# Three one-pass products of 12-bit halves in place of Strassen's scheme, in a state-space layer followed by a low-rank mixer

## The chip, the cores and the metric

The kernel runs on one core of a Trainium2 chip. The metric is the device time of one execution in microseconds; the median of three runs is given. Times inside an execution come from the hardware profiler, counted from the first instruction.

## The reference

Four batches, eight heads, 768 tokens, head size 32, state size 16. The first part is a chunked state-space scan, the second a mixer over tokens and then over channels (256 wide, inner width 1024):

```
for c in range(nc):                      # chunks of tokens
    M = einsum(C, B) * L                 # L = causal decay, exp(cum_i - cum_j)
    y = M @ x + (C @ state) * exp(cum)
    state = exp(sum la) * state + sum(B * x * decay)
x = y transposed to (batch, tokens, 8*32)
u = x + (x^T @ U @ V)^T                  # low-rank mixing over tokens, rank 32
out = u + max(u @ w_ch1, 0) @ w_ch2      # up, relu, down
```

All is in single precision; the weights U, V, w_ch1 and w_ch2 arrive as 64-bit floats.

## The kernel before, in words

Tokens are taken in pairs of 128-token chunks: 12 pairs `k`, three to a batch (`pairs`, `NPR` = 3). For a pair, `prep` (VectorE) and `decayed` (GpSimd) scale B and C by decays, `turning` transposes them on TensorE, `gram` forms C times B, `mask` (VectorE) applies the causal mask, `intra` and `inter` form y, `state` and `update` carry the state, and `yout` copies y to `yT`, channels by tokens. `ytokening` transposes it back for `project`, whose matmuls are at L595; `mixed` (L606, sums at L610) adds the token mixing to `yT` in place, so that `yT` then holds u.

The two channel products, up (1024 x 256 weight) and down (256 x 1024), are full single-precision matmuls. For batch 0 up is plain (`up`, L710) and the first third of down too (`whole`, L825). For the others both follow Strassen's scheme with seven products per 2 x 2 block: `quad` (L642) multiplies 128 x 128 weights by 384 columns; `down` (L750) multiplies 128 x 128 by 128, four to a product, with u added by transposes against the identity (L746, L819). Sums of the inputs are VectorE's (L617, L621, L739, and `operands` L1017 for the weights), partial results are copied aside by ScalarE (`kept`, L647, L756) and added by VectorE (L651, L764); relu is L630, L685, L715.

The 64-bit weights are turned to single precision by `to_fp32` (L324 to L336): two bit operations `e` and `top` on VectorE, two on ScalarE (`rest`, `power`), then three on VectorE (`rest`, `power`, `w`). Each weight chunk has 512 columns (the first two 256), nine for the two channel weights after one for U and V. `convert` and `convert_ahead` place these pieces between the up products of batch 0.

Nothing is reordered by a scheduler: `manual_schedule` leaves each engine the order in which the program issues. In step k of the main loop (L1032) the up pieces, down pieces and transposes of `plan` and `downs` run first, then `inter(k)`, `gram(k+1)`, `intra(k)`, `state(k+1)`, `mask(k+1)`, `inter`, `yout(k)`, `update(k+1)`. Batch b is projected at k = 3b + 3. All loads are on SP's queue, x and bc in six buffers, the weight words in six. Banks of the accumulator memory are handed out in rings of two under four tags:

```
BANKS = {"w": 2, "x": 2, "z": 2, "y": 2}
```

Of the kernel before, what the change touches and what calls it, by code (L numbers as in the profile page):

```python
# [11 lines left out]
UINT32 = mybir.dt.uint32  # L12
WCOLS = 512
NWORDS = 6
# [6 lines left out]
def kernel(  # L21
# [28 lines left out]
    P = 128  # L50
# [10 lines left out]
    HT = HS // P  # L61
# [5 lines left out]
    raw = ctx.enter_context(tc.tile_pool(name="raw", bufs=6))  # L67
# [40 lines left out]
    x_sb, bc_sb, paced = {}, {}, []  # L108
# [7 lines left out]
    def load_bc(k, blocks=(0, 1)):  # L116
        b, q = pairs[k]
        if k not in bc_sb:
            bc_sb[k] = raw.tile([P, 2, 2, NH, N], FP32, tag="bc", name="bc")
        for c in blocks:  # L120
            for i, src in enumerate((B, C)):
                paced.append(nc.sync.dma_start(
                    out=bc_sb[k][:, i, c],
                    in_=src[b, :, ts(2 * q + c, P), :].rearrange("h s n -> s h n")))

    def load_x(k, blocks=(0, 1)):
        b, q = pairs[k]
        if k not in x_sb:
            x_sb[k] = raw.tile([P, 2, NH, D], FP32, tag="x", name="x")
        for c in blocks:  # L130
            paced.append(nc.sync.dma_start(
                out=x_sb[k][:, c],
                in_=x[b, :, ts(2 * q + c, P), :].rearrange("h s d -> s h d")))
# [6 lines left out]
    w1 = const.tile([P, NCB, DF], FP32)  # L140
    w2 = const.tile([P, NM, DM], FP32)

    w2b = [[w2[:, half * NM // 2:(half + 1) * NM // 2, ts(n, P)] for n in range(2)]
           for half in range(2)]
    w2s = [const.tile([P, NM // 2, P], FP32, name=f"w2s{i}") for i in range(4)]
    weights = []

    def words_of(dst):
        p, i, j = dst.shape
        t = raw.tile([P, 2 * WCOLS], INT32, tag="words", name="words", bufs=NWORDS)  # L150
        weights.append((dst, t[:p, :2 * i * j]))
        return t[:p, :2 * i * j]

    def load_words(dst, src):

        p, i, j = dst.shape
# [4 lines left out]
    for k in range(NPR):  # L161
# [4 lines left out]
        if k:  # L166
            load_x(k)
    t = words_of(UV)
# [6 lines left out]
    eighths = words_of(w1[:, :, :quarter])  # L175
    weights.pop()
    for k in range(2):
        dst, t = w1[:, :, ts(k, P)], eighths[:, ts(k, 2 * NCB * P)]
# [3 lines left out]
    held += [load_words(w1[:, :, ts(k, quarter)], w13[:, :, ts(k, 2 * quarter)])  # L182
# [3 lines left out]
    for m in range(0, NM, 2):  # L186
        load_words(w2[:, m:m + 2],
                   w22[m * P:(m + 2) * P].rearrange("(m p) d -> p m d", p=P))
    for k in range(NPR + 1, NB * NPR):
        del paced[:-2]  # L190
        load_bc(k)
        load_x(k)
        if k > NPR + 3:
            for i in range(2, len(paced)):
                hold(paced[i], paced[i - 2])


# [110 lines left out]
    def to_fp32(dst, words):  # L308

        p, i, j = dst.shape
# [3 lines left out]
        def tmp(name, dtype):  # L318
            t = att.tile([P, WCOLS], dtype, tag=name, name=name)
            return t[:p, :i * j]  # L320

# [13 lines left out]
                                       op0=ALU.bitwise_and, op1=ALU.bitwise_or)  # L335
        nc.vector.scalar_tensor_tensor(  # L336
            out=dst, in0=rest.rearrange("p (i j) -> p i j", i=i), scalar=2.0 ** -20,
            in1=power.bitcast(FP32).rearrange("p (i j) -> p i j", i=i),
            op0=ALU.mult, op1=ALU.mult)
        yield  # L340

# [209 lines left out]
    def yout(k):  # L551
        b, q = pairs[k]
        if q == 0 and b:
            yT[b] = mix.tile([P, NCB, S], FP32, tag="yT", name="yT")
            ytok[b] = mix.tile([P, NC, DM], FP32, tag="ytok", name="ytok")
# [27 lines left out]
    def mixer(b):  # L583
        uT = yT[b]
        pT = mix.tile([P, P], FP32, tag="pT", name="pT")
        gT, hold, relus = {}, {}, []
# [14 lines left out]
        def mixed():  # L601
# [6 lines left out]
            for q in (0, 2, 1, 3):  # L608
                u = block(q // 2, q % 2)
                nc.vector.tensor_tensor(out=u, in0=h[q][:, :HS], in1=u, op=ALU.add)  # L610
            t = hold["t"] = [mix.tile([P, HS], FP32, tag=f"t{i}", name=f"t{i}",
                                      bufs=2 if i == 2 else 1) for i in range(4)]
            for i, (l, r) in enumerate((
                    (block(0, 1), block(0, 0)), (block(1, 1), t[0]),
                    (block(0, 1), block(1, 1)), (t[1], block(1, 0)))):
                if b:
                    nc.vector.tensor_tensor(out=t[i], in0=l, in1=r, op=ALU.subtract)  # L617

        def difference():

            nc.vector.tensor_tensor(out=hold["t"][2], in0=block(0, 1), in1=block(1, 1),  # L621
                                    op=ALU.subtract)
# [4 lines left out]
        def relu(n=None):  # L627
            for _ in range(len(relus) if n is None else min(n, len(relus))):
                g = relus.pop(0)
                nc.scalar.activation(g, g, AF.Relu)  # L630

        def quad(i):

            X = {}
            if i == 0:
                for k in range(2):
                    gT[k] = mix.tile([P, NM, HS], FP32, tag="gT", name="gT")

            def times(name, tag, lhsT, rhs, start=True):
                if start:  # L640
                    X[name] = bank(tag, HS)
                nc.tensor.matmul(out=X[name], lhsT=lhsT[:, ts(i, P)], rhs=rhs, start=start,  # L642
                                 stop=True, skip_group_check=True)

            def kept(name, of):
                X[name] = att.tile([P, WCOLS], INT32, tag=name, name=name).bitcast(FP32)[:, :HS]
                behind.setdefault("part", nc.scalar.copy(out=X[name], in_=X[of]))  # L647

            def out(k, half, of, other):
                g = gT[k][:, half * NM // 2 + i]  # L650
                nc.vector.tensor_tensor(out=g, in0=X[of], in1=X[other], op=ALU.add)  # L651
                relus.append(g)

            def p1():
                times("x", "x", w1[:, 0, :DF // 2], block(0, 0))
                kept("e", "x")
                relu(1)

            def p5():
                times("y", "z", ws[:, 0], hold["t"][0])  # L660
                kept("power", "y")
                relu(1)

            def p2():
                times("z", "z", w1[:, 1, :DF // 2], block(1, 0))
                out(0, 0, "z", "e")

            def p6():
                times("x", "x", ws[:, 1], hold["t"][1], False)
                kept("top", "x")  # L670
                relu(1)

            def p3():
                times("y", "z", ws[:, 3], block(1, 1), False)
                out(1, 0, "y", "top")

            def p7():
                times("x", "x", ws[:, 2], hold["t"][2], False)
                out(1, 1, "x", "power")

            def p4():
                times("x", "x", ws[:, 4], hold["t"][3], False)
                if i == 3:
                    relu()
                nc.vector.tensor_relu(gT[0][:, NM // 2 + i], X["x"])  # L685

            return dict(zip((1, 5, 2, 6, 3, 7, 4), (p1, p5, p2, p6, p3, p7, p4)))

        def two(i):

            q, r = quad(i), quad(i + 1)
            start = [q[1], q[5], q[2], q[6], q[3], None] if i else [
                q[1], q[5], None, q[6], q[3], q[2]]
            return start + [q[7], r[1], r[5], q[4], r[6], r[3], None, r[7], r[2], None, r[4]]

        def quads():

            q = [quad(i) for i in range(NM // 2)]
            when = {1: 0, 5: 1, 6: 3, 3: 4, 2: 5, 7: 6, 4: 9}
            order = sorted((7 * i + t, i, m) for i in range(NM // 2) for m, t in when.items())  # L700
            order = [q[i][m] for _, i, m in order]
            order.insert(2, None)
            return order

        def up(k, m):
            if m == 0:
                gT[k] = mix.tile([P, NM, HS], FP32, tag="gT", name="gT")
            g = bank("xz"[k if b == 0 else m % 2], HS)
            for n in range(NCB):
                nc.tensor.matmul(out=g, lhsT=w1[:, n, ts(m, P)], rhs=uT[:, n, ts(k, HS)],  # L710
                                 start=(n == 0), stop=(n == NCB - 1))
            if m % 2 and b:
                nc.vector.tensor_relu(gT[k][:, m], g)
            else:
                nc.scalar.activation(gT[k][:, m], g, AF.Relu)  # L715

        def down(j):

            X, S = {}, []

            def blocks():
                return [[gT[k][:, half * NM // 2:(half + 1) * NM // 2, ts(j, P)]
                         for half in range(2)] for k in range(2)]

            def sums(lo=0, hi=NM // 2, which=range(4), flush=True):
                if flush:
                    relu()
                if not S:
                    for _ in range(2):
                        t = raw.tile([P, 2 * WCOLS], INT32, tag="words", name="words",  # L730
                                     bufs=NWORDS).bitcast(FP32)
                        S.extend(t[:, ts(v, NM // 2 * P)].rearrange("p (i t) -> p i t", t=P)
# [379 lines left out]
```

## Time and profile before

| | us |
|---|---|
| median of three runs (238.43 to 241.82) | 239.74 |
| span of the profiled execution, first to last instruction | 237.3 |
| TensorE busy in it | 227.2 |
| TensorE weight loads busy (beside the products) | 175.1 |
| VectorE busy | 154.1 |
| ScalarE busy | 95.9 |
| GpSimd busy | 20.0 |

The profile gives no time of the profiled execution other than its span. PE is TensorE, PEld its weight loads, DVE VectorE, ACT ScalarE, POOL GpSimd, SP the queue that issues transfers. A line in a timeline begins with its start in us and the duration in us, then engine, source line, operation, output and inputs, shape and count; in brackets stands how long the engine was idle before and what ended the wait. Durations of neighbours overlap, so the distance between starts is the price of an instruction in a stream. A matmul in single precision leaves two records.

### The profile page before, as it was taken

To read this page: it belongs to the slowest core of one execution; us is meant where nothing else is said; L and a number is where in the kernel's file an instruction comes from. 1 tells how busy PE (TensorE), PEld (TensorE's weight loads), DVE (VectorE), ACT (ScalarE), POOL (GpSimd) and SP (SyncE) were. 2 spreads that over 40 slices of the span, in tenths; PEclk is the share of its full clock that TensorE was granted. 3 is DMA by queue.
4 is the path that set the end of the run, shared out by engine and by line. 5 is a ranking of instruction groups with operands and counts; after the bars stand their busy time and mean duration, and the time that the engine had idled before them with its cause. 6 is when DMAs were issued, how large, how long until landed. Compare 5 with 4: busy or idle time off the path is not lost.

```text
span 237.3 us, 7378 instructions
## 1 busy us (share of the span) xinstructions
PE 227.2 (96%) x3166; PEld 175.1 (74%) x3166; DVE 154.1 (65%) x363; ACT 95.9 (40%) x247; POOL 20.0 (8%) x40
## 2 busy tenths in 40 slices
PE   7699899997999999999999999999999999999995
PEld 5367556664878988565799987565799896559994
DVE  3666899878798575576896572566965362478411
ACT  5435658674705212456514112466312014652110
POOL 4221001122020200011012000010000000000000
PEclk9979999997999999999999999999999999999999
DMA  5985969996455556600001011000001001000111
GB/s 77 112 98 145 276 79 337 136 116 77 63 53 71 70 59 72 179 3 3 3 3 48 4 44 44 4 3 0 3 3 47 28 18 44 0 0 3 44 47 46
DMA packets 81909, 14.60 MB, mean 62 GB/s; under 512 B 76052, under 2 KB 80084, under 8 KB 81876
## 3 DMA queue, kind: packets, MB, share of 16 engines
q1 hardware_dynamic: 81876, 14.13, 32.6%
q8 instruction: 25, 0.41, 0.7%
q14 instruction: 8, 0.07, 0.1%
HBM read 10.98 MB, written 3.15 MB: 60 GB/s over the span
## 4 chain that ended last, share of the span: by engine, by line
PE 88%; DVE 5%; SPq 2%; DMA 1%; issue 1%; ACT 1%; DVEq 0%; ACTq 0%
PE x L750 17%; PE x L642 14%; PE z L750 13%; PE z L642 10%; PE x L710 5%; PE z L710 5%; PE y L546 3%; PE y L524 3%; PE x L414 2%; PE x L825 2%; PE w L566 2%; PE w L595 2%; PE w L447 2%; PE w L383 1%; DMA bc<-in_C_dram 1%; DVE M L426 1%
## 5 line engine op out<-in xcount | busy, mean ns | idle before, releaser
L642 PE MATMUL x<-t,ws 128*128 128x384 f32 x72 | 28.7, 496 | 0.0
L750 PE MATMUL x<-w2s,words 128*128 128x128 f32 x176 | 23.3, 276 | 0.0
L750 PEld LDWEIGHTS x<-w2s,words 128*128 128x128 f32 x176 | 21.6, 193 | 0.0
L630 ACT ACTIVATE gT<-gT 128x384 f32<-128x384 f32 x36 | 19.0, 528 | 2.4 <-DVE gT L651 2.3
L474 POOL TENSOR_TENSOR Sm<-S,slot 128x256 f32<-128x256 f32 (+1 forms) x12 | 8.8, 731 | 120.3 <-DVE S L467 89.2
L642 PEld LDWEIGHTS x<-t,ws 128*128 128x128 f32 x72 | 12.5, 190 | 8.0 <-ACT top L647 1.3
L739 DVE TENSOR_TENSOR words<-gT 128x512 f32<-128x512 f32 (+1 forms) x28 | 16.7, 597 | 0.6 <-ACT gT L630 0.6
L651 DVE TENSOR_TENSOR gT<-z,top 128x384 f32<-128x384 f32 x12 | 6.7, 558 | 15.2 <-PE z L642 13.4
L647 ACT COPY e<-x 128x384 f32<-128x384 f32 x12 | 5.7, 478 | 23.1 <-PE x L642 23.1
L808 ACT COPY o<-x 128x128 f32<-128x128 f32 x11 | 2.9, 265 | 28.6 <-PE x L750 28.6
L426 DVE TENSOR_TENSOR M<-x,causal 128x256 int32<-128x256 int32 x23 | 8.7, 419 | 8.6 <-PE z L414 7.3
L710 PE MATMUL x<-yT,w 128*128 128x384 f32 x32 | 13.2, 539 | 0.6 <-DVE yT L610 0.6
L558 ACT COPY yT<-y 128x256 f32<-128x256 f32 x24 | 7.8, 376 | 13.9 <-PE y L524 13.9
L467 DVE SCALAR_TENSOR_TENSOR S<-S,kept,w 128x64 f32<-128x64 f32 x40 | 11.2, 279 | 2.6 <-PE w L447 0.8
L353 DVE TENSOR_TENSOR BC<-bc,F 128x512 f32<-128x512 f32 (+1 forms) x15 | 9.2, 621 | 5.4 <-DMA bc<-in_C_dram 3.6
L750 PE MATMUL x<-w,gT 128*128 128x128 f32 x88 | 12.6, 286 | 0.0
L685 DVE TENSOR_SCALAR gT<-x 128x384 f32<-128x384 f32 x12 | 6.7, 557 | 9.1 <-PE x L642 9.1
L750 PEld LDWEIGHTS x<-w,gT 128*128 128x128 f32 x88 | 10.8, 191 | 2.3 <-issue 1.6
L710 PE MATMUL z<-yT,w 128*128 128x384 f32 x32 | 12.1, 504 | 0.0
L750 PE MATMUL z<-w2s,words 128*128 128x128 f32 x88 | 11.9, 279 | 0.0
L524 PE MATMUL y<-T,Sm 32*64 32x64 f32 x352 | 11.2, 233 | 0.7 <-ACT settled L480 0.4
L750 PE MATMUL z<-w,gT 128*128 128x128 f32 x88 | 11.6, 276 | 0.0
(186 smaller groups left out, 503.2 us busy)
## 6 DMA issues: line engine op xcount, KB each, us to landing
words<-in_moe_w_ch_dram SPq DMA_DIRECT2D x7, 512.0 KB, 5.9
x<-in_x_dram SPq DMA_DIRECT2D x24, 128.0 KB, 3.5
out_dram<-o SPq DMA_DIRECT2D x11, 256.0 KB, 2.1
bc<-in_B_dram SPq DMA_DIRECT2D x24, 64.0 KB, 2.9
bc<-in_C_dram SPq DMA_DIRECT2D x24, 64.0 KB, 2.8
words<-in_moe_w_ch_dram SPq DMA_DIRECT2D x2, 256.0 KB, 4.0
words<-in_moe_V_dram SPq DMA_DIRECT2D x1, 192.0 KB
words<-in_moe_U_dram SPq DMA_DIRECT2D x1, 192.0 KB, 5.2
```

The lines of the kernel that those rows point to most:

```text
L353: nc.vector.tensor_tensor(out=st[k]["BC"][:, :, c:c + n].rearrange("p i c h n -> p i (c h) n"), in0=bc_sb[k][:, :, c:c + n].rearrange("p i ...
L426: done = nc.vector.tensor_tensor(out=M[:, r].bitcast(INT32).rearrange("p c s i -> p (c s) i"), in0=g[r].bitcast(INT32).rearrange("p c s i ...
L467: done = nc.vector.scalar_tensor_tensor(out=new, in0=st["S", b], scalar=kept[:, b, j, None], in1=add, op0=ALU.mult, op1=ALU.add)
L474: nc.gpsimd.tensor_tensor(out=s["Sm"][:, sl], in0=s["S"][:, sl].rearrange("p i (s d) -> p i s d", s=2), in1=slot[:, None, :, None].to_broa ...
L524: product = nc.tensor.matmul(out=y[p][ts(r % 2, H), r // 2, c], lhsT=own[ts(r, Q)], rhs=s["T"][ts(r, Q), 1, c, ts(p, H)], start=fresh(k, p ...
L546: nc.tensor.matmul(out=y[p][ts(i, Q), n, c], lhsT=x_sb[k][half, c, h], rhs=s["M"][half, h // 2, c, h % 2], start=fresh(k, p, [i]), stop=Tr ...
L558: nc.scalar.copy(out=yp[:, :, :, p], in_=st[k]["y"][p])
L630: nc.scalar.activation(g, g, AF.Relu)
L642: nc.tensor.matmul(out=X[name], lhsT=lhsT[:, ts(i, P)], rhs=rhs, start=start, stop=True, skip_group_check=True)
L710: nc.tensor.matmul(out=g, lhsT=w1[:, n, ts(m, P)], rhs=uT[:, n, ts(k, HS)], start=(n == 0), stop=(n == NCB - 1))
L739: nc.vector.tensor_tensor(out=S[v][:, lo:hi], in0=l[:, lo:hi], in1=r[:, lo:hi], op=op)
L750: nc.tensor.matmul(out=X[name], lhsT=lhsT[:, i], rhs=rhs[:, i], start=start and u is None and i == 0, stop=True, skip_group_check=True)
```

## The change

Strassen's scheme goes, with all its sums. Each operand of the up and down products is held as three arrays in a reduced single-precision type: `near` (the upper 12 bits), `low` or `far` (the remainder, scaled or not) and `both` (a combination of the two). A product is a sum of three products near x near, low x far, both x both, with the accumulator scaled by 1 + 2^-12 on ScalarE between the first two and the third. Tokens are taken in blocks of 256, three to a batch: `split(j)` makes the three arrays of u, `up(j, i)` two of eight row blocks, `down(j)` 256 tokens of output. Weight conversion gets a fourth and fifth step, `weight(c)` runs steps 3 and 4 of chunk c, steps 1 and 2 of chunk c+1, then step 5 of chunk c. x and bc have four buffers instead of six, words eleven, and x and bc of step k+4 are loaded in step k.

```diff
-NWORDS = 6
+NWORDS = 11
+NEAR = 1.0 - 2.0 ** -13
+EPS = 2.0 ** -12
...
-    raw = ctx.enter_context(tc.tile_pool(name="raw", bufs=6))
+    raw = ctx.enter_context(tc.tile_pool(name="raw", bufs=4))
...
-    w1 = const.tile([P, NCB, DF], FP32)
-    w2 = const.tile([P, NM, DM], FP32)
+    w1 = [const.tile([P, NCB, DF], FP32R, name=f"w1{i}") for i in range(3)]
+    w2 = [const.tile([P, NM, DM], FP32R, name=f"w2{i}") for i in range(3)]
...
+        if parts:
+            near, low, both = parts
+            far = wide(tmp("top", FP32))
+            nc.scalar.activation(near, w, AF.Copy, scale=NEAR)
+            nc.gpsimd.tensor_tensor(out=far, in0=w, in1=near.bitcast(FP32), op=ALU.subtract)
+            yield
+            nc.scalar.activation(low, far, AF.Copy, scale=1.0 / EPS)
+            nc.vector.scalar_tensor_tensor(out=both, in0=near.bitcast(FP32), scalar=-EPS,
+                                           in1=far, op0=ALU.mult, op1=ALU.add)
+            yield
...
+        def split(j):
...
+            nc.scalar.activation(parts[0], u, AF.Copy, scale=NEAR)
+            nc.gpsimd.tensor_tensor(out=parts[1], in0=u, in1=parts[0].bitcast(FP32),
+                                    op=ALU.subtract)
+            nc.vector.scalar_tensor_tensor(
+                out=parts[2], in0=parts[1].bitcast(FP32), scalar=-1.0 / EPS,
+                in1=parts[0].bitcast(FP32), op0=ALU.mult, op1=ALU.add)
...
+        def scaled(t):
+            nc.scalar.activation(t, t, AF.Copy, scale=1.0 + EPS)
...
+            def first():
+                X["t"] = bank("xz"[i % 2], 2, W)
+                for m in range(2):
+                    products(X["t"][:, m], terms(2 * i + m, (0, 1)), m == 0)
+                scaled(X["t"])
+
+            def second():
...
+                for m in range(2):
+                    products(t[:, m], terms(2 * i + m, (2,)), False)
+                near, far, both = [g[:, ts(i % 2, 2)] for g in gs[j, i // 2]]
+                nc.scalar.activation(near, t, AF.Relu, scale=NEAR)
+                nc.vector.scalar_tensor_tensor(out=far, in0=t, scalar=0.0, in1=near.bitcast(FP32),
+                                               op0=ALU.max, op1=ALU.subtract)
+                nc.vector.scalar_tensor_tensor(
+                    out=both, in0=far.bitcast(FP32), scalar=-1.0 / EPS, in1=near.bitcast(FP32),
+                    op0=ALU.mult, op1=ALU.add)
...
+        def down(j, tag="z"):
...
+            def first(k):
+                if k == 0:
+                    X["t"] = bank(tag, 2, DM)
+                products(X["t"][:, k], terms(k, (0, 1)), k == 0)
+                if k:
+                    scaled(X["t"])
+            def second():
...
+                    products(t[:, k], terms(k, (2,)), False)
+                o = mix.tile([P, 2, DM], FP32, tag="o", name="o")
+                nc.scalar.copy(out=o, in_=t)
...
+            return lambda: first(0), lambda: first(1), second
...
+    split(0)
+    weight(1)
+    weight(2)
...
+    ups[0, 0][0]()
+    weight(3)
+    ups[0, 0][1]()
+    ups[0, 1][0]()
...
+        if k == NPR:
+            pieces = ([lambda: weight(6), ups[1, 0][0], lambda: weight(7), ups[1, 0][1],
+                       ups[1, 1][0], lambda: weight(8), ups[1, 1][1]] + turns[:2]
+                      + [lambda: weight(9)] + turns[2:])
...
+        elif q == 0:
...
+            pieces = ([d[0]] + tokens + [d[1], project] + turns[:2]
+                      + [mixed, lambda s=split: s(0), d[2]] + turns[2:] + u)
+        else:
...
+            pieces = ([lambda s=split, q=q: s(q)] if k > NPR + 2 else []) + (
+                [d[0]] + tokens + [d[1], u[0], d[2]] + u[1:-3] + turns[:2] + u[-3:-1] + turns[2:]
+                + u[-1:])
...
+        load(k + NPR + 1)
...
+    for j in range(1, NBL):
+        split(j)
+        d = downs[j - 1]
+        u = staggered([ups[j, i] for i in range(NQ)])
+        run([d[0], u[0], d[1], u[1], u[2], d[2]] + u[3:])
+    run(downs[NBL - 1])
```

`staggered` orders four up units as f0, f1, s0, f2, s1, f3, s2, s3, where f is a unit's `first` and s its `second`; d[0], d[1], d[2] are the three parts of a down block.

## The prediction

> **What bounds the kernel now.** I read the chain of waits first, then the page's slices, then the stages by windows, then the pitches in the timelines.
>
> The chain of waits, by engine:
>
> ```profile
> PE 88%; DVE 5%; SPq 2%; DMA 1%; issue 1%; ACT 1%; DVEq 0%; ACTq 0%
> ```
>
> TensorE sets the end; but a share is a mean over stages. The slices show where that is close:
>
> ```profile
> PE   7699899997999999999999999999999999999995
> DVE  3666899878798575576896572566965362478411
> PEclk9979999997999999999999999999999999999999
> ```
>
> In slices 6 to 14 (30 to 83 us) VectorE is as full as TensorE. The windows from the end of batch 0's token mixing, cut where loop steps k=3 and k=6 begin, then at the three projections (L595), say it in microseconds (window, length, then PE, PEld, DVE, ACT, POOL busy, clock, DMA):
>
> ```profile
> 29.40:51.70 22.30, 21.69 (x140) 13.62 (x141) 19.57 (x44) 15.59 (x35) 2.43 (x4) 1.00 0.90 173
> 51.70:75.40 23.70, 21.99 (x530) 17.07 (x528) 20.72 (x44) 10.83 (x26) 3.67 (x4) 0.93 0.57 68
> 79.75:132.25 52.50, 52.49 (x784) 41.32 (x788) 36.25 (x82) 20.13 (x52) 4.40 (x6) 1.00 0.28 48
> 132.25:183.54 51.29, 51.23 (x714) 39.82 (x718) 29.88 (x69) 17.50 (x46) 1.14 (x2) 1.00 0.05 18
> 183.54:237.30 53.76, 50.91 (x380) 42.05 (x379) 25.37 (x56) 15.49 (x42) 0.00 (x0) 1.00 0.08 25
> ```
>
> First two rows: VectorE 88% busy with the weights' conversion. Last three: TensorE alone, VectorE 47 to 69%. The change takes work off TensorE everywhere and adds VectorE, ScalarE and GpSimd work, so the two halves must be costed apart.
>
> TensorE's pitch is the distance between starts (up, down, transpose):
>
> ```profile
> 205.68 1.45 PE L642 MATMUL x<-t,ws 128*128 128x384 f32 x4
> 206.97 0.81 PE L642 MATMUL z<-yT,ws 128*128 128x384 f32 x2
> 217.01 1.06 PE L750 MATMUL z<-w,words 128*128 128x128 f32 x8
> 217.90 0.27 PE L746 MATMUL x<-ident,yT 128*128 128x128 f32 x1
> 218.01 1.06 PE L750 MATMUL x<-w2s,words 128*128 128x128 f32 x8
> ```
>
> A product has two records: 384 columns 1.29/4 = 322.5 ns each, 128 columns 0.89/8 = 111.7. A transpose is one, 110 ns. The line through both is 6 ns + 0.823 ns a column and record, so 2 clocks of 2.4 GHz a record and 4 a product. Loading 128 columns of weights shows in neither, so it is hidden.
>
> VectorE in one quarter of the first weight (512 columns):
>
> ```profile
> 33.06 0.42 DVE L324 TENSOR_SCALAR e<-words 128x512 int32<-128x512 int32 x1
> 33.40 0.42 DVE L326 TENSOR_SCALAR top<-words 128x512 int32<-128x512 int32 x1
> 33.73 0.68 DVE L332 SCALAR_TENSOR_TENSOR rest<-top,rest 128x512 f32<-128x512 f32 x1
> 34.33 0.68 DVE L334 SCALAR_TENSOR_TENSOR power<-words,power 128x512 int32<-128x512 int32 x1
> 35.05 0.69 DVE L336 SCALAR_TENSOR_TENSOR w<-rest,power 128x512 f32<-128x512 f32 x1
> 35.66 0.42 DVE L324 TENSOR_SCALAR e<-words 128x512 int32<-128x512 int32 x1
> ```
>
> Start to start: 0.34, 0.33, 0.60, 0.72, 0.61, together 2.60 us; a two-source instruction on 512 floats is priced 0.62. For 256 columns the same view gives 1.55 and 0.35. GpSimd's two-source instruction at 128, 192 and 256 columns:
>
> ```profile
> 14.40 0.40 POOL L365 TENSOR_TENSOR bd<-bc,FD 128x128 f32<-128x128 f32 x1 [0.65 <-DMA bc<-in_B_dram]
> 21.81 0.51 POOL L474 TENSOR_TENSOR Sm<-S,slot 128x192 f32<-128x192 f32 x1 [2.73 <-DVE S L467]
> 18.46 0.61 POOL L474 TENSOR_TENSOR Sm<-S,slot 128x256 f32<-128x256 f32 x1 [1.90 <-DVE S L467]
> ```
>
> Estimate from these for 512: 0.61 + 256 x 1.7 ns = 1.05 us; beside a busy VectorE the 256 form takes 1.06 (65.65), so up to 1.8.
>
> **The Trainium skill.** "FP8 and Floating Point Precision", TensorE Precision Notes: true FP32 takes four passes, reduced precision reads the float and truncates it. Four clocks a column agree; no row here shows the reduced form. "TensorE: Matmul & The Clock Gate", Back-to-back issue gap: N/2.4 + 2.5 ns for one pass, 109 ns at 256. The same page says the clock halves after idling; here, after 1.29 us without work at 54.13, four L710 records took 2.72 us instead of 1.29. "VectorE: DVE Perf Modes", the errata section: (N+151)/0.96, 691 ns for a two-source fp32 instruction of 512; L332 and L336 last 680 to 690.
>
> **The change, part by part.**
>
> *TensorE.* One pass over 256 columns, by my line at one clock: 6 + 256 x 0.412 = 111 ns (bounds: 107 of pure streaming; 216 at two clocks a column). An up block is 8 row blocks x 3 x 2 = 48 products, a down block 2 x 3 x 8 = 48: 5.33 us each. A batch of three blocks: 32.0 plus 12 transposes 1.3 = 33.3. Now it is 28 x 0.645 + 84 x 0.2234 + 1.3 = 38.2. It saves 4.9 a batch; batch 0 (32 x 0.645, 16 x 0.433, 56 x 0.2234, transposes) saves about 8. All: 22.7 us.
>
> *VectorE after the mixing.* Up to the end of the last conversion its queue holds: mixing sums 4 x 0.47 = 1.9; two splits 1.2; two 256 chunks 3.8 less 0.4 done before, seven 512 chunks x (2.60 + 0.62 for `both`) = 22.5; six up units x two evacuations x 0.62 = 7.4; `keep` 0.9; three `prep` 1.8; one `mask` (4 x 0.34) and one `update` 2.5. That is 41.6 us of pure occupation. It leaves out Strassen's operands and sums, which lay later. (Before, the conversion stood in the same queue with no evacuations: relu was ScalarE's.)
>
> *New waits.* `both` waits for `far` on GpSimd, which waits for `near` on ScalarE: 0.64 (L1019) + 1.05 + two handovers of 0.1 = 1.9. Only `e` and `top` of the next chunk (0.67) stand between, so VectorE idles 1.2 in each of six chunks, 1.9 in the last, 0.8 and 0.6 in the halves: 10.5. Behind the waiting `both` stand the evacuations of the up products, and TensorE waits for those through the banks. `split(0)`: 1.1. An evacuation's `near` is queued on ScalarE behind `low`, which waits for GpSimd too: 0.5 x six units = 3.0. Sum 14.6.
>
> *Stage sums* against the profiled 237.3. Mixing at 29.4, unchanged. Then 41.6 + 14.6 = 56.2: 85.6. The first down product needs the last chunk's `low`; ScalarE's `settled` and VectorE's mask stand before it: 86.7. Before, this point (k=4) was 56.15; TensorE had hidden there. k=4: down 5.33 + 0.44, two up units 2.67, four token and four turn transposes 0.88, attention 2.65 (154.51 to 157.16), waits 1.3 (`gram` 1.1 and a scaling 0.2, below): 13.3. k=5: 5.77 + 5.33 + 0.88 + 2.65 + 1.3 = 15.9. k=6 to the projection: 4.0. Waking the clock: 1.7. Together 34.9, and the projection of batch 1 comes at 121.6 instead of 79.75.
>
> Each later batch: 51.9 (mean of two windows) - 4.9 + new waits. These are, each step: `gram`'s fourth bank is freed by the last unit's `near` and `far` (0.55 + 0.62 + handovers, less `inter` 0.37), 1.1 where it is 0.4 now: 0.7 x 3. Mixing to the first up product: two sums 0.94, `near` 0.6, GpSimd 1.05, handovers 0.3, under a cover of 2.4 (d2 and turns), 0.8, and 0.4 for pT. The last `second` of a block follows its scaling by 0.44 only: 0.2 to 0.3 x 3. Together 4.0. Two batches 2 x 51.0 = 102.0: 223.6. In the other steps `split` stands on GpSimd behind `Sm` and `bd` (0.61 each): by the step's start plus 3.7 it is done, and the first up product comes 4.0 after it, behind d0, tokens and d1: nothing, and up to 1 us a step if GpSimd runs at its slow rate.
>
> The tail from the last projection: 1.45 + 0.45 + 0.87, d2 2.2, split 0.8, three ups 16.0, three downs 17.3, waits 3.6 (scaling before the last d2 0.8, splits and g 2.8), copy 0.5, store 2.1, handovers 0.3: 45.6, against 53.8 now. End: 269.2.
>
> *At nothing:* x and bc prefetched by four buffers instead of six, loads moved into the loop on SP behind the stores: k+4 is asked for two steps of 15 us before `prep`, landing is 3.5 us. If that cover goes (a store ahead of it waits for its copy), 3.5 a step. The words no longer wait for six buffers, which takes away waits of 2.3 us for bc.
>
> The median of the runs shown lies 2.4 above the span (the page has no other time of that execution), so 271.6.
>
> **Rivals.**
> *Handovers pace the ups.* An up unit is 1.33 on TensorE, 1.24 on VectorE and about 1.0 on ScalarE. If PSUM-sourced evacuations cost 0.70, VectorE needs 1.4; with the scaling's latency each of 36 units gains 0.4: 285. For: the three are nearly level. Against: downs stand between most of them.
> *The waits hide.* All the new ones (14.6, 8.0, 3.6 and 4.3 in k=4 and k=5) at zero: 238.7 + 2.4 = 241. For: TensorE is in order but deep. Against: VectorE and ScalarE run in order too and nothing stands between.
> *Not one pass.* At 216 ns, 1152 x 0.105 = 121 us, of which the six units under the conversion hide 30: 362. No row excludes it.
> *TensorE stays the bound (faster).* Place: the 29.4 to 86 stretch. If VectorE's queue did not count there, 237.3 - 22.7 + 2.4 = 217. It decides once the conversion ends 31.9 earlier, near 54; VectorE's 41.6 us of instructions end at 71 without any wait, so they would have to cost 40% less than measured.
>
> **The numbers.** My forecast 0.60 (own range 258 to 284), handovers 0.22, waits hidden 0.08, not one pass 0.05, TensorE-bound 0.05. By a bound of 2% (about what a measurement of this kernel tells from no change): faster 0.05, within 0.08, slower 0.87. Range 252 to 290: it leaves out the last three, 0.18.
>
> **What would show it.** Records of 256 columns one per product at about 111 ns; the first L595 after batch 0's at 118 to 125; VectorE waiting for GpSimd's `far` about 1.2 us per chunk; TensorE half idle from 35 to 87; later projections 51 apart. A first projection below 100 proves the conversion's price wrong; 45 apart, the waits.

## The result, and the profile after

| | us |
|---|---|
| median before (four runs) | 239.81 |
| median after (300.11 to 303.39) | 302.57 |
| ratio, with its 95% interval | 1.263 (1.254 to 1.273) |
| span of the profiled execution, before and after | 237.3 and 301.0 |

Some executions take over 1.5% longer than the fastest of their kernel, and the medians here and below leave those out. The kernel is slower, as forecast, but by 63 us instead of 32, and 13 us above the range. The slices after, and the chain of waits by engine:

```profile
PE   8988265653343988989989899699898989999994
DVE  4675766667667226073393664735619172555450
PEclk9999557565555695988999999999799999999999
PE 51%; DVE 17%; SPq 11%; ACT 10%; POOL 4%; issue 4%; DMA 2%; POOLq 0%; ACTq 0%; DVEq 0%
```

TensorE was 88% of the chain and is 51%. From slice 5 to 13 (30 to 98 us) it is mostly a third to two thirds busy, and its clock is at 0.5 to 0.7. VectorE is not full there either, 6 or 7 tenths: the two wait for each other. Here are the same stages as before, by windows (from the mixing to the first down product, from there to the projection of batch 1, then from projection to projection and to the end):

```profile
29.60:98.85 69.25, 32.21 (x313) 25.97 (x313) 45.46 (x89) 31.60 (x62) 15.25 (x15) 0.56 0.42 70
98.85:141.54 42.69, 38.97 (x543) 36.25 (x541) 17.21 (x34) 15.68 (x33) 5.88 (x7) 0.83 0.26 39
141.54:197.96 56.42, 51.38 (x846) 46.52 (x845) 31.22 (x60) 24.39 (x49) 8.27 (x9) 1.00 0.21 35
197.96:252.06 54.10, 50.32 (x775) 45.79 (x774) 26.84 (x50) 22.18 (x43) 4.93 (x5) 0.97 0.05 17
252.06:301.00 48.94, 42.93 (x377) 39.55 (x376) 21.25 (x31) 20.29 (x36) 3.84 (x3) 1.00 0.07 23
```

The projection of batch 1 comes at 141.5 instead of 79.75: 61.8 of the 63.7 us (about 8 us less of batch 0's down products are left by then than before). The two periods are 3.9 and 2.8 longer, the tail 4.9 shorter.

Inside the first window, one quarter of a weight on VectorE, the conversion's `far` on GpSimd, and the next evacuation:

```profile
39.06 0.69 DVE L338 SCALAR_TENSOR_TENSOR rest<-top,rest 128x512 f32<-128x512 f32 x1
39.66 0.68 DVE L340 SCALAR_TENSOR_TENSOR power<-words,power 128x512 int32<-128x512 int32 x1
40.38 0.69 DVE L343 SCALAR_TENSOR_TENSOR e<-rest,power 128x512 f32<-128x512 f32 x1
...
43.12 0.69 DVE L354 SCALAR_TENSOR_TENSOR w<-w,top 128x512 fp32r<-128x512 f32 x1 [1.38 <-POOL top L351]
44.27 0.69 DVE L676 SCALAR_TENSOR_TENSOR words<-x,words 128x512 fp32r<-128x512 f32 x1 [0.46 <-ACT words L675]
...
41.81 1.27 POOL L351 TENSOR_TENSOR top<-e,w 128x512 f32<-128x512 f32 x1 [3.13 <-ACT w L350]
```

`both` (L354) stood waiting 1.38 us for GpSimd, as the forecast's 1.2 said; GpSimd took 1.27 for 512 columns instead of the 1.05 drawn on from narrower ones. The next lines show the products' pitch in a dense stretch at the end, and the same sixteen down products in step k=4 and near the end:

```profile
286.05 1.11 PE L645 MATMUL x<-u,w 128*128 128x256 f32 x8
287.00 1.58 PE L645 MATMUL z<-u,w 128*128 128x256 f32 x12
288.41 0.63 PE L645 MATMUL x<-u,w 128*128 128x256 f32 x4
...
98.85 3.78 PE L645 MATMUL x<-w,words 128*128 128x256 f32 x16
...
250.06 2.07 PE L645 MATMUL x<-w,words 128*128 128x256 f32 x16
```

There is one record a product, at 1.41/12 = 117.5 ns (113 to 118 in other dense stretches): one pass, as the change says. At 98.85 sixteen of them took twice as long, after the clock had fallen in the idle start. The largest sum of waits on TensorE, the longest single ones on it, and VectorE's for GpSimd (waiter, what it waited for, sum, times, longest):

```profile
PE z L430 <- DVE words L676: 12.7, 8, 3.7
PE x L645 <- ACT w L350: 9.7, 3, 5.5
DVE w L354 <- POOL top L351: 12.3, 9, 2.1
```

The first is `gram` waiting for the bank of the last up unit, in eight steps; the second are three up units of batch 0 waiting for `near` of their weights.

SP's queue has 11% of the chain instead of 2%. The moved loads do not explain the loss: SP's part of the chain ends at 49 us, no load in the list of waits holds TensorE after the first microseconds, and VectorE waited for loads 0.5 us in all (3.6 before).

### The profile page after: what moved, and what is told of

Its sections match the earlier page's. It is cut to its first block, busy times and chain, and to the rows that moved or that the text cites. A ratio compares the mean times of both kernels' runs of the same rounds, so it can differ in the third digit from the quotient of the medians.

```text
span 301.0 us, 7915 instructions
## 1 busy us (share of the span) xinstructions
PE 241.5 (80%) x3438; PEld 211.9 (70%) x3438; DVE 158.7 (53%) x322; ACT 128.0 (43%) x262; POOL 44.6 (15%) x61
## 4 chain that ended last, share of the span: by engine, by line
PE 51%; DVE 17%; SPq 11%; ACT 10%; POOL 4%; issue 4%; DMA 2%; POOLq 0%; ACTq 0%; DVEq 0%
PE x L645 30%; SPq L129 8%; PE z L645 8%; DVE words L676 5%; DVE words L678 4%; ACT words L675 3%; POOL top L351 3%; PE y L562 2%; DMA bc<-in_C_dram 2%; PE z L430 2%; ACT z L650 2%; POOL u L636 2%; SPq L138 2%; PE y L540 1%; SPq L164 1%
## 5 line engine op out<-in xcount | busy, mean ns | idle before, releaser
L645 PE MATMUL x<-w,words 128*128 128x256 f32 x576 | 82.5, 294 | 1.3 <-issue 1.1
L645 PEld LDWEIGHTS x<-w,words 128*128 128x128 f32 x576 | 73.8, 197 | 3.1 <-issue 1.2
L645 PE MATMUL x<-u,w 128*128 128x256 f32 x288 | 48.5, 306 | 21.2 <-ACT w L350 9.7
L645 PEld LDWEIGHTS x<-u,w 128*128 128x128 f32 x288 | 40.7, 205 | 25.4 <-ACT w L350 10.8
L645 PE MATMUL z<-u,w 128*128 128x256 f32 x288 | 46.6, 305 | 7.2 <-ACT z L650 3.7
L645 PEld LDWEIGHTS z<-u,w 128*128 128x128 f32 x288 | 40.1, 205 | 10.7 <-ACT z L650 6.2
L676 DVE SCALAR_TENSOR_TENSOR words<-x,words 128x512 fp32r<-128x512 f32 x24 | 16.6, 691 | 57.5 <-ACT words L675 57.5
L650 ACT ACTIVATE x<-x 128x512 f32<-128x512 f32 x36 | 21.0, 584 | 44.4 <-PE x L645 44.4
L678 DVE SCALAR_TENSOR_TENSOR words<-words 128x512 fp32r<-128x512 f32 x48 | 35.4, 736 | 1.6
L430 PE MATMUL z<-Cm,T 32*64 32x128 f32 x184 | 14.2, 339 | 12.7 <-DVE words L676 12.7
L676 DVE SCALAR_TENSOR_TENSOR words<-z,words 128x512 fp32r<-128x512 f32 x24 | 16.5, 688 | 9.2 <-ACT words L675 9.1
L430 PE MATMUL x<-Cm,T 32*64 32x128 f32 x184 | 17.2, 336 | 0.2
L351 POOL TENSOR_TENSOR top<-e,w 128x512 f32<-128x512 f32 (+1 forms) x9 | 10.4, 1153 | 35.6 <-ACT w L350 35.6
L708 ACT COPY o<-x 128x512 f32<-128x512 f32 x12 | 7.0, 586 | 19.1 <-PE x L645 19.1
```

The source lines that it names most:

```text
L351: nc.gpsimd.tensor_tensor(out=far, in0=w, in1=near.bitcast(FP32), op=ALU.subtract)
L430: nc.tensor.matmul(out=g[r][cols, c], lhsT=s["T"][rows, 0, c, cols], rhs=s["Cm"][rows, :, c, cols], start=(c == 0), stop=True, skip_group_ ...
L645: nc.tensor.matmul(out=t, lhsT=lhsT, rhs=rhs, start=start, stop=True, skip_group_check=True)
L650: nc.scalar.activation(t, t, AF.Copy, scale=1.0 + EPS)
L676: nc.vector.scalar_tensor_tensor(out=far, in0=t, scalar=0.0, in1=near.bitcast(FP32), op0=ALU.max, op1=ALU.subtract)
L678: nc.vector.scalar_tensor_tensor(out=both, in0=far.bitcast(FP32), scalar=-1.0 / EPS, in1=near.bitcast(FP32), op0=ALU.mult, op1=ALU.add)
```

## The experiments

My theory after the result was that the start is a chain of handovers in which VectorE waits, TensorE idles and its clock falls, and that the later steps wait for the evacuation. The rival was that products and evacuations simply cost more than forecast. Each run below begins with its median; the kernel before stood at 236.7 to 239.3 beside these runs.

Positions come from one profiled execution each. In these the mixing itself began anywhere from 28.6 to 35.6 us, at code that the edits leave alone. So they are counted from the first sum of the mixing, which stands at 29.56 in the changed kernel. "d0" is the first down product (69.3 on this count) and "P1" the projection of batch 1 (112.0). A period is the time from one projection to the next.

**No split of the weights.**

```diff
-    w1 = [const.tile([P, NCB, DF], FP32R, name=f"w1{i}") for i in range(3)]
+    w1 = [const.tile([P, NCB, DF], FP32R, name="w1")] * 3
...
-            near, low, both = parts
-            far = wide(tmp("top", FP32))
-            nc.scalar.activation(near, w, AF.Copy, scale=NEAR)
...
-            nc.scalar.activation(low, far, AF.Copy, scale=1.0 / EPS)
```

> The weights are not split: near, low and both are one array, so the fourth and fifth conversion steps (ScalarE, GpSimd, VectorE) are left out and the products are of other numbers. Theory start (the chain of ScalarE, GpSimd and VectorE per weight chunk sets the time up to the first down product): VectorE loses 12.3 us of waits and 5 us of instructions, the first down product comes 17 us earlier than 98.9, near 82, the clock recovers sooner, total 280 to 286. Theory products (the pitch of 118 ns and the evacuations set the time, the start only shows it): total within 5 us of 302.

278.4; d0 50.2, P1 88.7. That is 24 us less. d0 comes 19.1 us sooner, and the stage from d0 to P1 is 4.2 us shorter at a clock of 0.96 instead of 0.83. The periods (55.4, 53.0) fell by 1 us each and the tail (49.1) stayed. So the split of the weights costs about 19 us in the start. But d0 in this kernel still comes 23 us later than the same point in the kernel before (26.8), so the split is not the only cost. VectorE waits here too, 6.1 us for ScalarE before the evacuations, whose `near` now stands behind the next chunk's `power`.

**`far` on VectorE.** `nc.gpsimd.tensor_tensor(out=far` becomes `nc.vector.tensor_tensor(out=far`.

> The subtraction that gives far in the conversion is VectorE's instead of GpSimd's. Theory start, handover form: a chunk's wait of 1.4 us goes, an instruction of 0.62 comes and about 0.1 of waiting for near remains, 0.7 us a chunk gained: 5 us earlier at the first down product, total about 297. If VectorE's amount of work and not the waiting set the start, 0.62 x 8 = 5 us are lost: 307.

303.0; d0 69.1, as good as unchanged. In this execution the mixing began 6.0 us later than in the changed kernel (35.58 instead of 29.56), before any edited instruction:

```profile
35.58 0.56 DVE L626 TENSOR_TENSOR yT<-x,yT 128x384 f32<-128x384 f32 x1 [2.89 <-PE z L622]
...
104.64 3.78 PE L645 MATMUL x<-w,words 128*128 128x256 f32 x16
...
DVE words L676 <- ACT words L675: 6.5, 6, 2.3
DVE top L351 <- ACT w L350: 5.8, 9, 0.7
```

VectorE's 12.3 us of waiting for GpSimd became 5.8 us of waiting for `near` (`e` and `top` no longer cover it), about 5 us of forming `far` itself, and 1.9 us more of waiting before the evacuations. So neither outcome came, 5 us sooner or 5 later. Not GpSimd is the price, but whatever stands between `w` and `both` with nothing beside it. The next stage, whose code is the same, took 3.9 us less at a clock of 0.95; why the clock stayed up there is not shown.

**Idle matmuls against the clock's fall.** `fill(12)` or `fill(16)` ahead of batch 0's up units and of `state(4)`, `fill(8)` ahead of `gram` at k=4 and 5.

> Idle matmuls are put before the up products of batch 0 and before the waits of steps k=3, 4 and 5, so that TensorE's clock does not fall; nothing else changes. Theory clock: steps k=4 and k=5 take 17.3 us each like the later ones instead of 18.6 and 19.8, and VectorE's wait for the decay products in the start shrinks: 4 to 6 us gained, total about 297. Theory start without the clock: 302, or some microseconds more where an idle matmul outlasts the wait it fills.

294.8; d0 68.6, d0 to P1 37.1 instead of 42.7, at a clock of 1.00 instead of 0.83. So about 5.6 us of this stage were the clock's. In the start the clock rose as well, from 0.56 to 0.82, and d0 came only 0.7 us sooner, so there it was not the price, or the idle matmuls took back what it gave. On the stage after d0 other runs agree: the stage took 38.2 us at 0.96 and 40.4 at 0.89, with its products unchanged.

**Early transposes.** This is the edit of the later steps; k=3 and k=4 are changed likewise.

```diff
-                [d[0]] + tokens + [d[1], u[0], d[2]] + u[1:-3] + turns[:2] + u[-3:-1] + turns[2:]
-                + u[-1:])
+                [d[0]] + tokens + [d[1], u[0]] + turns + [d[2]] + u[1:])
```

> The transposes of the pair after next, and with them ScalarE's copies T and Cm (1.3 us), are placed ahead of the last up units of a step instead of between their parts. Theory: gram waits for the last unit's evacuation because its near stands behind T and Cm on ScalarE; at k = 4, 5, 7, 8 gram comes 1.2 us sooner, and at k=3 state no longer waits 4.2 us for Cm: 6 to 9 us gained, total 294 to 296. Rival: the last evacuation is late because VectorE paces the units (1.42 us each against 1.41 on TensorE): less than 2 us gained.

297.9, between the two expectations; but `gram`'s waits for VectorE fell only from 12.7 to 11.5, and 2.5 us of the gain lie where the granted clock was higher (0.87 instead of 0.83 between d0 and P1, 1.00 instead of 0.97 in the second period). VectorE's queue shows why the early transposes helped `gram` so little (`far` L676, `both` L678):

```profile
164.59 0.69 DVE L676 SCALAR_TENSOR_TENSOR words<-x,words 128x512 fp32r<-128x512 f32 x1 [4.75 <-ACT words L675]
165.32 0.69 DVE L678 SCALAR_TENSOR_TENSOR words<-words 128x512 fp32r<-128x512 f32 x1
165.99 0.69 DVE L676 SCALAR_TENSOR_TENSOR words<-z,words 128x512 fp32r<-128x512 f32 x1
166.72 0.69 DVE L678 SCALAR_TENSOR_TENSOR words<-words 128x512 fp32r<-128x512 f32 x1
```

It runs without a gap from the first unit on, a unit in 1.33 to 1.40 us, and is idle 4.75 before. TensorE issues a unit in 1.36 to 1.41 with four in a row, so VectorE's tail reaches into `gram`. As to `gram`, the rival of this run stands.

**VectorE's order.** Early transposes; `both` of a unit issued after the next unit's `far`; `u[1], u[2]` ahead of `d[2]`.

> The early transposes of the run before, and on VectorE each unit's both is issued after the next unit's far (the last one after mask), and the last part of a down block goes after the first unit's second instead of before it. Theory (VectorE's two instructions a unit, 1.42 us, are what gram waits for): gram's wait falls from 1.2 to 4 us a step to under 1, in the steps k = 5 to 10, 8 to 10 us gained over the early transposes alone: 288 to 290. Rival (TensorE's own work fills the step and gram's wait is only its end): under 2 us.

295.4; d0 66.4, d0 to P1 38.2 (67.6 and 41.4 in the run before). The periods are 55.6 and 52.5 instead of 56.1 and 52.9 there: 1.0 us, where 8 to 10 were expected in the steps k=5 to 10. The 3.2 us between d0 and P1 come with the clock, 0.96 instead of 0.87. TensorE is busy 49.2 of 52.5 us in the second period, so little is left for the order of VectorE to give.

**No third product.** Both x both is left out in up and down.

> The third product of up and down (both x both) is left out, 384 of 1152 matmuls of 118 ns, 45 us of TensorE; all evacuations stay. If TensorE sets the later steps, the distance between projections falls by 96 x 118 ns = 11.3 us from 55.3 to 44, and the total by about 38. If VectorE's evacuations set them, units come at 1.42 us of VectorE whatever TensorE does, and the distance falls by half of that or less.

292.3, in one execution; the others took 297.1 to 300.1, and the profile is of one of these. The mean clock was 0.80 to 0.81 in all of them (0.86 to 0.89 in the changed kernel). There are ninety-six products less in a batch, and the periods are 57.8 and 53.3. Their window lines:

```profile
137.77:195.53 57.76, 48.64 (x750) 43.29 (x749) 30.98 (x60) 23.76 (x49) 8.23 (x9) 0.79 0.21 34
195.53:248.87 53.34, 42.52 (x679) 37.90 (x678) 26.66 (x50) 20.96 (x43) 4.96 (x5) 0.87 0.05 16
```

Work of 11 us a batch was taken from TensorE and its clock fell to 0.79 and 0.87. `gram`'s waits for VectorE in the two periods rose from 5.2 to 13.1 us. This run therefore does not say what the steps would cost at the full clock; it shows that most of a gain on TensorE can be lost to waits and clock, 10 us of an expected 38 being left.

**No third array from the evacuation.** VectorE's L678 is left out; down reads `far` in its place.

> The evacuation's third array is not formed: VectorE's second instruction of each up unit (48 x 0.72 = 35 us) is left out, and the third down product reads far in its place. If VectorE paces the units, each later step is 2 us shorter, the distance between projections falls by 5 to 6 us and the first down product comes up to 6 x 0.7 = 4 us sooner: 282 to 286. If TensorE sets the steps: within 4 us of 302.

290.8; d0 66.3, d0 to P1 37.9, periods 55.4 and 51.2. The largest part of the gain, 4.8 us, lies between d0 and P1 at a clock of 0.96; the periods fell by 1.0 and 2.9 us where 5 to 6 were expected, and 1.2 of the second is the clock's.

**The fifth conversion step late.**

```diff
     def weight(c):
-        convert(c, 2)
+        convert(c)
+        if c > 1:
+            convert(c - 1)
+        convert(c)
         convert(c + 1, 2)
-        convert(c)
```

> A chunk's fifth conversion step (low, both) is issued after the third step of the next chunk, so that the 2.3 us of ScalarE and GpSimd lie beside 1.9 us of VectorE's work of the next chunk; the up products follow one chunk later. Theory start by waits: VectorE's 12.3 us of waits for far go, the first down product comes 9 to 12 us sooner, near 88: total 290. If the work and the TensorE ends of the chain set the start: under 4 us gained.

293.9; d0 56.9, 12.4 us sooner:

```profile
34.63 0.56 DVE L626 TENSOR_TENSOR yT<-x,yT 128x384 f32<-128x384 f32 x1 [3.04 <-PE z L622]
...
91.55 3.78 PE L645 MATMUL x<-w,words 128*128 128x256 f32 x16
...
DVE w L354 <- POOL top L351: 1.4, 1, 1.4
```

VectorE's waits for `far` fell from 12.3 to 1.4 us, with the same arithmetic. The expected 9 to 12 us came, and they are the clearest proof that these waits were on the path. As in the run with `far` on VectorE, the mixing began later in the profiled execution, here by 5.1 us.

**All cures together; the same without the split.**

> All cures together: late fifth conversion step, idle matmuls in the waits of the start, early transposes, far ahead of both on VectorE, and a down block's last part behind the first unit's second. If their gains add (8.7, 4.7, 7.1): 282. If the clock's part is shared between them (each shortens the same idle stretches): 284 to 288.

> As the run before, but with the weights not split (near, low and both one array, other numbers), so with no conversion steps four and five at all. Theory start: the first down product near 76, the projection of batch 1 near 112, total 268 to 272, which leaves 30 us over the kernel before to the evacuations of batch 0 on VectorE and to its up and down products, which no longer lie under the conversion. If splitting were the whole cause of the slowdown: near 245.

287.6 and 282.1. In both, several of the idle matmuls had come to stand in the chain of waits, 1.9 to 5.5 us each, so neither says what the cures are worth. Without them:

> The combined cures (late fifth step, early transposes, far ahead of both, down's last part later) without any idle matmuls after the mixing. If the idle matmuls cost more than the clock gives: 280 to 284, the first down product near 85. If the clock is worth more: 290.

> The weights are not split (near, low and both one array, other numbers), early transposes, far ahead of both, no idle matmuls. Theory start: 5 to 8 us below the 282.1 with idle matmuls, 274 to 277. If the clock is worth as much as they cost: 282.

284.8 (d0 56.4, P1 96.8) and 279.1 (d0 51.0, P1 89.3). The cures give 18 us of the 63, 12.9 of them at d0, about what the late fifth step gives alone. Without the split the other cures give nothing that can be told apart (278.4 with the split alone gone).

**Conversion beside more of TensorE's work.** The last two chunks are converted in step k=4; the attention of pair 3 and two up units lie beside them, and both first down blocks follow in k=5.

```diff
         elif k == NPR + 1:
+            pieces = (tokens + [ups[1, 2][0], lambda: weight(8),
+                                ups[1, 3][0]] + turns + [lambda: weight(9), ups[1, 2][1],
+                                ups[1, 3][1], lambda: convert(9), lambda: split(2)])
```

> The combined cures, and the last two weight chunks are converted in step k=4 instead of k=3, with the attention of pair 3, the tokens of pair 3 and the up units 1,2 and 1,3 of batch 0 beside them; both first down blocks then follow in step k=5 (twelve word buffers, one pT). Theory serial start (TensorE's work of batch 0 stands behind the conversion): about 7 us of attention and up products move under the conversion, the projection of batch 1 comes near 122 instead of 128.9, total 281. Rival (VectorE's queue is full, what is put beside the conversion only delays it): within 2 us of 287.6.

290.0, again with idle matmuls on the chain (four of 4 to 5 us). Without them, with the split and without it:

> The same with the last two chunks converted in step k=4 and both first down blocks in step k=5, without idle matmuls. Theory serial start: 5 to 7 us below the run before, 274 to 278. Rival (VectorE's queue is full): equal to it within 2 us.

> The overlapped start of e2 and the weights not split (other numbers). What is left over the kernel before is then the evacuations of batch 0 on VectorE, the order, and the later steps. By VectorE's sum (41.6 less 5.0 of both, 36.6, plus k=4's) the projection of batch 1 comes at 105 to 112, total 260 to 268.

285.3 and 274.6. With the split, the reordering gives nothing (284.8 before it). VectorE's queue was already full: it is busy 55.4 of the 64.4 us to the first down product, 86% (87% before the reordering, 66% in the changed kernel):

```profile
29.60:94.01 64.41, 35.92 (x496) 29.65 (x496) 55.36 (x97) 35.78 (x75) 19.35 (x18) 0.69 0.49 80
```

Without the split it gives 4.5 us (279.1 to 274.6). So the serial order costs only once VectorE has room. What is left in the last kernel is large: P1 at 85.9 against 50.3 before, and 35 us in all. It lies in batch 0's evacuations and in the order, or in both; these runs do not take them apart.

**What the pitch is made of.** Each product of 256 columns as two of 128, and as four of 64.

```diff
-                nc.tensor.matmul(out=t, lhsT=lhsT, rhs=rhs, start=start, stop=True,
...
+                for c in range(2):
+                    nc.tensor.matmul(out=t[:, ts(c, P)], lhsT=lhsT, rhs=rhs[:, ts(c, P)],
...
```

> Each product of 256 columns is issued as two of 128 with the same weights; all else stays. Three readings of the pitch of 118 ns: if it is streaming of one clock a column plus about 11 ns, a product of 128 takes 64 and the total rises by about 2304 x 64 - 1152 x 118 = 12 us less what is hidden; if it is the loading of weights, 128 columns take 118 too and the total rises by about 100; if narrow products of this type run at several clocks a column, they take 200 or more.

> Each product of 256 columns is issued as four of 64 with the same weights. If the loading of 128 columns of weights is the floor, each takes 112 ns at the full clock as with 128 columns. If narrow products stream at two clocks a column, they take 58 ns.

456.9 and, in a single execution, 1107.3. TensorE near the end of each:

```profile
385.28 1.95 PE L646 MATMUL x<-u,w 128*128 128x128 f32 x16
387.06 1.95 PE L646 MATMUL z<-u,w 128*128 128x128 f32 x16
```

```profile
1087.69 7.02 PE L646 MATMUL x<-w,words 128*128 128x64 f32 x32
1094.52 0.69 PE L704 MATMUL x<-ident,yT 128*128 128x128 f32 x2
PEclk8555555555565555555555555555555555555555
```

128 columns take 1.78/16 = 111 ns at the full clock. 64 take 6.83/32 = 213 ns at half the clock, which would be 107 at the full one if it scales with it. So 64 columns are no cheaper than 128, and hardly cheaper than 256: these products have a floor of about 107 to 111 ns. Had 64 columns cost half as much as 128 at the same clock, they would have taken about 111 ns here, so a fixed price a column is refuted. Loading 128 columns of weights fits that floor; it was not measured apart from the product.

## Why the prediction was wrong

The direction and the place held, and so did the mechanism in the main: the conversion on VectorE with its waits sets the start, TensorE idles there, and the later batches gain nothing. The step that failed is the list of waits in the stage sums. It put at nothing VectorE's waits for TensorE and for the second split, and it put the clock's price once where its cause came back. Against the forecast's 269.2 the profiled execution is 31.8 us longer, and 12.0, 7.8, 5.4, 3.1 and 3.3 of these lie in the start, from d0 to P1, in the two periods and in the tail.

- *Mixing to d0*: 57.3 forecast, 69.3 measured. Of the 66.9 us up to the end of the last conversion (29.56 to 96.44), VectorE waited for 22.5 (14.6 forecast) and was occupied for the other 44.4 (41.6 forecast). Its waits in this stage:

```profile
DVE w L354 <- POOL top L351: 12.3, 9, 2.1
DVE words L676 <- ACT words L675: 4.6, 5, 2.7
DVE u L638 <- POOL u L636: 3.2, 2, 2.0
DVE own L307 <- PE w L303: 2.5, 1, 2.5
```

  Waiting for `far` was priced nearly right (10.5), and behind `low` the evacuations waited 1.8, less than the 3.0 set. At nothing had stood the second split (2.0, behind `Sm` on GpSimd), the decay products (2.5, on TensorE behind an up unit that waits for `low`; 0.9 without the split) and the last up unit of block 0 (2.7, on TensorE behind `gram` and `state`). The run without the split says the same from the other side: the forecast's price of the split was 18.5 (5.0 for `both`, 10.5, 3.0), and 19.1 came. The miss lies in what stays without it.
- *d0 to P1*: 34.9 forecast, 42.7 measured. The clock's recovery stood at 1.7, and with the clock held up the stage takes 37.1, so the clock cost about 5.6. It fell to half twice more, at 113 and 134 us of the profile, where `gram` had waited 2.5 and 1.3. These two waits were set at 1.1 each, and the pitch is 1.3 of the stage.
- *The pitch*: 111 forecast, 117.5 measured, about 7 us over 1152 products, nearly all outside the start. One point of the forecast's line, 128 columns at 111.7, stands at the floor found above, so that line could not tell streaming from loading. What makes 256 columns 6 ns dearer than the floor is open.
- *The periods*: 51.0 forecast, 56.4 and 54.1 measured. The pitch gives 1.9 of each. One pause for which the profile names no cause gives 1.1 of the first (192.36 to 194.24). A fall of the clock in the second gives 1.2: without it the period is 52.9, as with early transposes. `gram` waited 3.4 and 1.8 us, about the 1.1 a step that was set, so the evacuation's tail was priced rightly. About 2 us of the first stay open.
- *The tail*: 45.6 forecast, 48.9 measured; 2.0 are the pitch, the rest was not looked into.

Of the rivals, "handovers pace the ups" came nearest in number (285), and a unit does take 1.40 on VectorE against 1.41 on TensorE. But it put its price on the units alone, while 20 of the 32 us lie before P1, so its number is not a proof of its reason. "Not one pass" and "TensorE stays the bound" are excluded by the pitch and by the start. "The waits hide" fell with the run that moved them: d0 came sooner by as much as they lasted. The best kernel with all arithmetic in place took 284.8, and no run beat the kernel before.

On the Trainium skill: "TensorE: Matmul & The Clock Gate", Back-to-back issue gap, gives N/2.4 + 2.5 for an isolated product and says that in a stream the weight load and the product together set the spacing. The forecast took the first, 109 ns, and left out the second; 117.5 was measured. The page's section on LDWEIGHTS gives P/1.2, 107 ns for 128 columns, which agrees with the floor found with 128 and 64 columns (111, and 213 at half the clock).

## What to carry to other kernels

When a change takes passes off TensorE and pays with splits on other engines, cost the stage in which those engines are already full first: there the saving is worth nothing and the payment is paid in whole (19.1 us here, where 18.5 were set). An array made by three engines in turn costs the handovers as well as the instructions, unless as much other work is queued between the turns; queueing it gave 12.4 us. List the waits for the relieved engine too, since it idles and its clock may fall, and ask after every long wait whether the clock's price comes again. When you compare two profiles, count from an event ahead of the edit: the mixing began up to 6 us later in some of these executions, enough to hide a gain of 5 or to feign a loss.

## What was not expected of the hardware

- The clock follows more than TensorE's busy share: in the kernel with 64 columns TensorE was 99.6% busy from 200 to 300 us at a clock of 0.50, and with 128 columns the stage from d0 to P1 ran 101 us at 0.50, 99% busy, and later ones at 0.90 to 0.99. What the clock follows instead is not shown.
- Idle matmuls put into waits to hold the clock gave 8 us in the changed kernel (302.6 to 294.8). In the combined kernel, where the waits were shorter, they became the chain themselves (five of 3.4 to 5.0 us), and the kernel without them was 2.7 us faster.
- GpSimd's subtraction took 1.27 us for 512 columns and 0.73 for 256; the forecast had drawn on another two-source instruction, which takes 0.61 for 256. Where VectorE's `top` fell beside that subtraction, in the run with the late fifth step, it took 1.5 us instead of 0.42, five times:

```profile
57.85 1.49 DVE L332 TENSOR_SCALAR top<-words 128x512 int32<-128x512 int32 x1
57.74 1.32 POOL L351 TENSOR_TENSOR top<-e,w 128x512 f32<-128x512 f32 x1 [3.67 <-ACT w L350]
```
